# First loads, gate products and value loads of a windowed attention in front of a mixture of experts: another order

## The chip, the cores and the metric

One core of one Trainium2 chip. The metric is the device time of one execution in microseconds (us). TensorE (PE; PEld is its weight load), VectorE (DVE), ScalarE (ACT), GpSimd (POOL) and SyncE (SP) each run their instructions in program order; SP issues all direct loads and stores of the stage that is changed. About 1% of the time is what a measurement of this kernel can tell from no change.

## The reference, cut to what matters

```python
scores = scale * np.matmul(q, k.transpose(0, 1, 3, 2))     # 8 batches, 8 heads, 576 positions, 64 per head
mask = (rel >= 0) & (rel < 64)                             # each position sees the 64 last ones
attn = softmax(np.where(mask, scores, -1e9))
x = np.matmul(attn, v)                                     # as 4608 tokens x 512
...
do_compute = x @ w_skip > 0
e_idx = np.argmax(x @ w_gate, axis=1)                      # one of 8 experts; gate_w is its softmax
y = gate_w * (np.maximum(x @ w1[e_idx], 0) @ w2[e_idx])    # per token
out = x + y where do_compute, else x
```

## The kernel before

The tokens are cut into 36 tiles of 128 (two blocks of 64 positions of one batch, or the ninth blocks of two batches). A loop over t = 0 to 36 with an order written out by hand (`tc.manual_schedule`) interleaves the steps of several tiles. What round t puts on the engines, in this order: the loads that `at[t]` names (SP); `score(t + 1)` (PE: 4 band matmuls, line 214, that put the mask into PSUM, then 32 small q·k matmuls, line 228); the gate steps that `gate_at[t]` names; `soften(t)` (DVE maximum, line 243, and subtraction, line 244, then the exponential on ACT, line 245); `tile_out(t - 2)`, which is `av_tile` (PE: 32 matmuls, line 338; DVE: four operations, lines 350 to 358; SP: stores, two tiles later); `transpose_p(t - 1)` (PE: 8 transposes, line 254; ACT: two copies, line 255); and the ACT copies that `lower_at[t]` names (line 316). `routes(1)`, three times a round, puts out steps of the choice of experts, which runs in groups of 8, 8, 6, 8, 4 and 2 tiles. Score tiles (`psc`) and the softmax tiles (`sp`) have two buffers each, and so has the PSUM tag "t" that transposes and gate products share.

Loads come in 16 groups n of two tiles; `first_of[n]` is the first tile of group n: 0, 2, 4, 6, 9, 11, 13, 15, 18 and so on (after every eight tiles there is one of ninth blocks, with loads of its own, the tails). A group is q (512 KiB), k (512 KiB, 640 for odd n), vT (512 KiB: v transposed, for the gate products) and vm (592 KiB: v for the weighted sum, with room for gate columns). Before, q and k of group n are issued at round first_of - 5 (`AHEADQ`), vT and vm at first_of - 4 (`AHEADV`), from n = 2 and n = 1 on; what would fall before round 0 is issued there. vT has two buffers (`NTB`), the others four.

The gate steps of a group: `gate_v(n)` multiplies vT with the gate weights (PE, line 288, then an ACT copy, line 290) at round first_of - 2; `gate_vt(n)` transposes that product (PE, line 296), copies it into vm (ACT, line 308), and lets POOL copy the upper half of vm down for the block before (line 309), at first_of - 1; `lower` copies what is left of it on ACT, at first_of - 1 and, for odd n, at first_of. Rounds 0 and 1 hold what would come earlier. `tile_out` of the group's first tile stands in round first_of + 2. The tails have a product, a transposition and two such copies at rounds 9m + 4 to 9m + 7.

Ahead of the loop stand the first loads, in this order (KiB): k and q of the first block pair 128 + 128, identb 32, band 64, the next 128 + 128, ident 64, wg 64, then vT of group 0 (512), vm of group 0 (592), the rest of group 0's k and q (256 + 256), k and q of group 1 (640 + 512), two constants (180 and 305). Round 0 adds group 1's vT and vm, group 2's vT and vm, and group 2's k and q.

After the loop, the tokens of each expert are gathered and two matrix products per expert run with operands split in two parts each (lines 655 to 657).

Of the kernel before, what the change touches and what calls it, by code (L numbers as in the profile page):

```python
# [20 lines left out]
P = 128  # L21
# [21 lines left out]

NQB, NKB, NVB, NTB, NSB, NPB, XPB = 4, 4, 4, 2, 2, 3, 4

AHEADQ, AHEADV = 5, 4
SDELAY = 2

NRAW, NEARLY = 6, 2
# [76 lines left out]
def window_attention_moe(ctx: ExitStack, tc, a, out):  # L126
# [26 lines left out]
    def load_constants():  # L153
        nc.sync.dma_start(cf, a["c_f"])
        nc.sync.dma_start(lists, a["c_list"])
        nc.gpsimd.memset(onesb, 1.0)
        nc.gpsimd.tensor_copy(trib, cf[:, off["tri"]])
        nc.gpsimd.tensor_copy(base, cf[:, off["base"]])
        nc.gpsimd.tensor_copy(ent[:, :, 0].bitcast(I32), cf[:, off["tid"]])
# [19 lines left out]
    def load_qk(n, parts=((0, 4),)):  # L179
        b, g = divmod(n, 2)  # L180
        if parts[0][0] == 0:
            qs[n] = qkp.tile([P, 4, 4, 64], F32, name="q", bufs=NQB)
        q, k = qs[n], ks[n % NKB]
        for s, e in parts:
            s0 = s + 1 if s or not g else 0
            nc.sync.dma_start(k[:, s0 : e + 1], a["kT"][b, :, 4 * g + s0 - 1 : 4 * g + e])
            nc.sync.dma_start(q[:, s:e], a["qT"][b, :, 4 * g + s : 4 * g + e])
# [50 lines left out]
    def soften(t):  # L238
        ps = ss[t]
        s = sp.tile([P, 2 * 4, P], F32, name="s")  # L240
        flat = ps.rearrange("p r h k -> p (r h) k")
        mx = sm.tile([P, 8], F32, name="mx", bufs=2)
        nc.vector.tensor_reduce(mx, flat, axis=AX.X, op=ALU.max)  # L243
        nc.vector.tensor_tensor(s, flat, mx.unsqueeze(2).to_broadcast([P, 8, P]), op=ALU.subtract)  # L244
        nc.scalar.activation(s, s, AF.Exp, scale=0.125)  # L245
        ss[t] = s

    def transpose_p(t):
        s = ss.pop(t)
        ptm = ptp.tile([P, 8, P], F32, name="ptm")  # L250
        for r in range(2):
            pt = psum.tile([P, 4, P], F32, name="pt", tag="t", bufs=2)
            for p in range(4):
                nc.tensor.transpose(pt[:, p], s[:, 4 * r + p], ident)  # L254
            nc.scalar.copy(ptm[:, 4 * r : 4 * r + 4], pt)  # L255
        pts[t] = ptm
# [2 lines left out]
    banks = {}  # L259
    vms = {}  # L260

    def load_v(n):


        b, g = divmod(n, 2)
        vm = vp.tile([P, 4, H, VW], F32, name="vm", bufs=NVB)
        vT = vtp.tile([P, 4, 256], F32, name="vT")
        nc.sync.dma_start(vT, a["vT"][b, g])
        nc.sync.dma_start(
            vm.rearrange("p (j z) h c -> p j z (h c)", z=2)[:, :, 1], a["vp"][b, :, 2 * g : 2 * g + 2]  # L270
        )
        if g == 0:
            nc.gpsimd.memset(vm[:64, 0], 0.0)
        vms[n] = vm, vT

    def load_v_tail(m):
        vt = vp.tile([P, 2, H, VW], F32, name="vt", bufs=1)
# [6 lines left out]
    def gate(vT, nt):  # L284

        pw = psum.tile([P, nt * P], F32, name="pw", tag="t", bufs=2, padded_shape=[P, 512])
        for p in range(4):
            nc.tensor.matmul(pw[32 * p : 32 * p + 32], wg[:, p], vT[:, p], start=True, stop=True)
        vw = vtp.tile([P, nt * P], F32, name=f"vw{nt}")
        nc.scalar.copy(vw, pw)  # L290
        return vw

    def gate_t(vw, nt):
        pk = psum.tile([P, nt, P], F32, name="pk", tag="t", bufs=2, padded_shape=[P, 4, P])
        for j in range(nt):
            nc.tensor.transpose(pk[:, j], vw[:, j * P : j * P + P], ident)
        return pk.rearrange("p n (h c) -> p n h c", c=16)[..., 0:9]

    def gate_v(n):
        vms[n] = vms[n][0], gate(vms[n][1], 2)  # L300

    def gate_vt(n):

        b, g = divmod(n, 2)
        vm, vw = vms[n]
        pg = gate_t(vw, 2)
        w = vm.rearrange("p (j z) h c -> p j z h c", z=2)
        nc.scalar.copy(w[:, :, 1, :, 65:74], pg)  # L308
        nc.gpsimd.tensor_copy(w[64:, :, 0], w[:64, :, 1])  # L309
        for j in range(2):  # L310
            vs[9 * (n // 4) + 2 * (n % 4) + j] = [vm[:, 2 * j], vm[:, 2 * j + 1]]

    def lower(n, j):

        before = vms[n][0][64:, 1] if j else vms[n - 1][0][64:, 3]
        nc.scalar.copy(vms[n][0][:64, 2 * j], before)

    def gate_tail(m):
        vms["t", m] = vms["t", m][0], gate(vms["t", m][1], 1)
# [6 lines left out]
        vs[9 * m + 8] = [vt[:, 0], vt[:, 1]]  # L326

    def tail_lower(m, z):
        nc.scalar.copy(vms["t", m][0][:64, z], vms[4 * m + 2 * z + 1][0][64:, 3])

    def av_tile(t, lh, sums):
        blks = tiles[t]
# [200 lines left out]
    def routes(n):  # L533

        for _ in range(n):
            if not late:
                return
            if held[0] == "sums":
                held[1] += 1
                if progress[0] < NT or held[1] < 3:  # L540
                    continue
            held[:] = next(late[0], late), 0
            if held[0] is late:
                late.pop(0)
# [247 lines left out]
    with tc.manual_schedule():  # L792
        load_qk(0, ((0, 1),))
        nc.sync.dma_start(identb, a["c_identb"])
        nc.sync.dma_start(band, a["c_band"])
        load_qk(0, ((1, 2),))
        nc.sync.dma_start(ident, a["c_ident"])
        nc.sync.dma_start(wg, a["wg"])
        load_v(0)
        load_qk(0, ((2, 4),))  # L800
        load_qk(1)
        load_constants()
        at = {}

        def when_at(t, f, n):
            at.setdefault(max(t, 0), []).append((f, n))

        gate_at, lower_at = {}, {}
        for n in range(NG):
            if n >= 1:  # L810
                when_at(first_of[n] - AHEADV, load_v, n)
            if n >= 2:
                when_at(first_of[n] - AHEADQ, load_qk, n)
            gate_at.setdefault(max(first_of[n] - 2, 0), []).append((gate_v, n))
            at_t = max(first_of[n] - 2, 0) + 1
            gate_at.setdefault(at_t, []).append((gate_vt, n))
            lower_at.setdefault(at_t, []).append((lower, n, 1))
            if n % 2:
                lower_at.setdefault(at_t + 1, []).append((lower, n, 0))
# [8 lines left out]
        for t in range(NT + 1):  # L828
            m, r = divmod(t, 9)
            for f, n in at.get(t, ()):  # L830
                f(n)
            if t + 1 < NT:
                score(t + 1)
            for f, n in gate_at.get(t, ()):
                f(n)
            rest = its[0].split(*xhl[0], XSPLIT.index(t), "t") if t in XSPLIT else None
            routes(1)
            if t < NT:
                soften(t)
            if t >= 2 and t < NT:  # L840
                tile_out(t - 2)
            if rest is not None:
                rest()
            routes(1)
            if t >= 1 and t < NT:
                transpose_p(t - 1)
            routes(1)
            for f, n, j in lower_at.get(t, ()):
                f(n, j)
            for _ in range(U0.count(t)):  # L850
                weight_dma_first()
            if t in USPLIT:
                weight_split(ptr["split"])
                ptr["split"] += 1
# [245 lines left out]
```

## Time and profile before

| what | value |
|---|---|
| time, median of 3 runs | 479.13 us (475.76 to 481.17) |
| the profiled execution's own time | 476.28 us |
| its span, first to last instruction | 474.6 us |
| busy share of PE, DVE, ACT, POOL | 88%, 63%, 46%, 26% |
| moved by DMA | 99.61 MB |

The profile is one execution. Busy shares are means over a stage of attention (to about 205 us), which is where the change lies, and a stage of experts behind it. Times in rows count from the first instruction. A row of the order of time gives start, duration, engine, line, operation, out<-in, count, and in brackets how long the engine was idle before it and what ended that.

### The profile page before, as it was taken

What the parts mean: (1) busy time and instruction counts of PE and PEld (TensorE: products, weight loads), DVE (VectorE), ACT (ScalarE), POOL (GpSimd) and SP (SyncE); (2) the same over time, 40 slices, a digit from 0 to 9 for tenths busy, and PEclk for the clock granted to TensorE, in tenths of its full rate; (3) what the DMA queues carried; (4) which work ended last, traced back from release to release, by engine and by line L of the source; (5) the groups of instructions that cost most, each with busy time, mean ns of one, the idle gap of its engine ahead of it and who ended that gap; (6) DMA issues with size and microseconds to landing.
All of it is one profiled execution on the core that took longest, in us unless ns stands there. A gap on an engine that the chain in (4) does not pass through costs nothing.

```text
span 474.6 us, 11307 instructions
## 1 busy us (share of the span) xinstructions
PE 418.2 (88%) x4510; PEld 344.8 (73%) x4510; DVE 299.4 (63%) x562; ACT 220.3 (46%) x365; POOL 124.5 (26%) x139
## 2 busy tenths in 40 slices
PE   2899887987988688487999999999999999999990
PEld 2577774875766566376899888898888889988660
DVE  2478974896696788479833658847365476656510
ACT  1387554754674466467313444443334244444410
POOL 4210226024407141503456302305005030101010
PEclk9999988898999799799999999999999999999997
DMA  7999999859994984458573662746447555755000
GB/s 240 402 374 412 344 316 278 275 199 231 260 385 127 309 312 126 61 187 237 157 239 72 226 220 68 273 133 205 165 144 246 162 178 191 233 189 175 0 27 18
DMA packets 36646, 99.61 MB, mean 210 GB/s; under 512 B 6014, under 2 KB 8062, under 8 KB 36576
## 3 DMA queue, kind: packets, MB, share of 16 engines
q1 hardware_dynamic: 31728, 89.25, 57.6%
q0 software_dynamic: 4864, 9.63, 5.9%
q8 instruction: 36, 0.59, 0.5%
q14 instruction: 18, 0.15, 0.1%
HBM read 84.76 MB, written 14.73 MB: 210 GB/s over the span
## 4 chain that ended last, share of the span: by engine, by line
PE 60%; DVE 9%; ACT 3%; issue 3%; another core or an unknown queue 2%; POOLq 0%; DVEq 0%; ACTq 0%
PE p L655 8%; PE p L657 8%; PE p L656 8%; PE yw L655 4%; PE yw L656 4%; PE yw L657 4%; PE av L338 3%; PE yv L655 3%; PE yv L657 3%; PE yv L656 3%; PE pt L254 2%; PE ps L228 2%; DVE wlo L608 2%; PE px L644 2%; PE yu L657 2%
## 5 line engine op out<-in xcount | busy, mean ns | idle before, releaser
L608 DVE TENSOR_TENSOR wlo<-raw,whi 128x1024 fp32r<-128x1024 f32 x72 | 87.7, 1222 | 17.6 <-ACT whi L607 15.9
L692 ACT ACTIVATE hh<-p 128x256 fp32r<-128x256 f32 (+6 forms) x72 | 27.7, 385 | 129.7 <-PE p L657 116.9
L655 PE MATMUL p<-xh,whi 128*128 128x256 f32 (+6 forms) x288 | 84.5, 294 | 1.6 <-DVE gds L432 1.1
L657 PE MATMUL p<-xh,wlo 128*128 128x256 f32 (+6 forms) x288 | 83.7, 291 | 0.7 <-DVE wlo L608 0.7
L656 PE MATMUL p<-xl,whi 128*128 128x256 f32 (+6 forms) x288 | 83.7, 290 | 0.1
L607 ACT CAST whi<-raw 128x1024 fp32r<-128x1024 f32 x72 | 74.4, 1043 | 0.0
L693 DVE SCALAR_TENSOR_TENSOR hl<-p,hh 128x256 fp32r<-128x256 f32 (+6 forms) x72 | 30.3, 420 | 69.9 <-ACT hh L692 62.5
L715 POOL DMA_INDIRECT out<-yo,les x18 | 18.8, 1046 | 156.2 <-DVE yo L714 143.7
L655 PEld LDWEIGHTS p<-xh,whi 128*128 128x128 f32 x288 | 54.5, 189 | 4.9 <-issue 1.3
L656 PEld LDWEIGHTS p<-xl,whi 128*128 128x128 f32 x288 | 54.5, 189 | 1.8 <-issue 0.4
L657 PEld LDWEIGHTS p<-xh,wlo 128*128 128x128 f32 x288 | 54.6, 189 | 0.9 <-DVE wlo L608 0.9
L245 ACT ACTIVATE s<-s 128x1024 f32<-128x1024 f32 x36 | 38.1, 1058 | 36.8 <-DVE s L244 32.5
L440 POOL DMA_INDIRECT lists<-ent,gdi x36 | 37.0, 1029 | 67.2 <-DVE gdi L438 58.6
L338 PEld LDWEIGHTS av<-vm,ptm 128*64 128x64 f32 x1024 | 40.2, 149 | 19.3 <-issue 11.7
L243 DVE TENSOR_REDUCE mx<-ps 128x8 f32<-128x1024 f32 x36 | 43.8, 1216 | 15.5 <-PE ps L228 15.5
L338 PE MATMUL av<-vm,ptm 128*64 128x74 f32 x1024 | 46.1, 246 | 8.5 <-issue 5.6
L228 PE MATMUL ps<-k,q 64*64 64x128 f32 x1024 | 44.8, 294 | 9.6 <-issue 5.6
L255 ACT COPY ptm<-pt 128x512 f32<-128x512 f32 x72 | 38.9, 584 | 23.2 <-remote 14.9
L228 PEld LDWEIGHTS ps<-k,q 64*64 64x64 f32 x1024 | 36.3, 146 | 16.6 <-issue 10.1
L244 DVE TENSOR_TENSOR s<-ps,mx 128x1024 f32<-128x1024 f32 x36 | 44.1, 1225 | 5.6 <-ACT s L245 0.8
L254 PE MATMUL pt<-ident,s 128*128 128x128 f32 x288 | 41.2, 285 | 3.1 <-ACT ptm L255 2.9
L309 POOL COPY vm<-vm 64x1184 f32<-64x1184 f32 x16 | 18.7, 1172 | 72.1 <-ACT vm L308 66.9
(150 smaller groups left out, 672.2 us busy)
## 6 DMA issues: line engine op xcount, KB each, us to landing
raw<-wq SPq DMA_DIRECT2D x72, 512.0 KB
vm<-vp SPq DMA_DIRECT2D x16, 592.0 KB
vT<-vT SPq DMA_DIRECT2D x16, 512.0 KB
out<-x SPq DMA_DIRECT2D x32, 256.0 KB
q<-qT SPq DMA_DIRECT2D x15, 512.0 KB
k<-kT SPq DMA_DIRECT2D x8, 640.0 KB
k<-kT SPq DMA_DIRECT2D x7, 512.0 KB
kt<-kT SPq DMA_DIRECT2D x8, 256.0 KB
```

The costliest lines, as they stand in the source:

```text
L228: nc.tensor.matmul(ps[64 * hf : 64 * hf + 64, r, p], q[h, p], k[h, :, p], start=False, stop=p == 3, skip_group_check=True,)
L243: nc.vector.tensor_reduce(mx, flat, axis=AX.X, op=ALU.max)
L244: nc.vector.tensor_tensor(s, flat, mx.unsqueeze(2).to_broadcast([P, 8, P]), op=ALU.subtract)
L245: nc.scalar.activation(s, s, AF.Exp, scale=0.125)
L254: nc.tensor.transpose(pt[:, p], s[:, 4 * r + p], ident)
L255: nc.scalar.copy(ptm[:, 4 * r : 4 * r + 4], pt)
L338: nc.tensor.matmul(av[64 * hf : 64 * hf + 64, h // 4, (h % 4) * VW : (h % 4 + 1) * VW], ptm[:, (h % 2) * 4 + h // 2, 64 * hf : 64 * hf + 6 ...
L607: nc.scalar.copy(hi, raw)
L608: nc.vector.tensor_tensor(lo, raw, hi.bitcast(F32), op=ALU.subtract)
L655: nc.tensor.matmul(o, lh, rh, start=first, stop=False)
L656: nc.tensor.matmul(o, lh, rl, start=False, stop=False)
L657: nc.tensor.matmul(o, ll, rh, start=False, stop=last)
```

## The change

The first loads are put in another order: the rest of group 0's q and k comes ahead of ident, wg and vT; group 1's q and k are loaded in two halves, in front of vm of group 0 and behind it; group 1's vT and vm follow. The POOL steps that prepare constants for the choice of experts move from the head to round 4. `gate_v` and `gate_vt`, with their `lower` copies, come a round later for every group; in round 0 they stand behind `soften`, in round 1 behind `transpose_p`, from round 2 on where they stood. From group 2 on vT and vm are issued a round later (first_of - 3).

```diff
--- before.py
+++ after.py
@@ -43,7 +43,7 @@
 
 NQB, NKB, NVB, NTB, NSB, NPB, XPB = 4, 4, 4, 2, 2, 3, 4
 
-AHEADQ, AHEADV = 5, 4
+AHEADQ, AHEADV = 5, 3
 SDELAY = 2
 
 NRAW, NEARLY = 6, 2
@@ -153,6 +153,8 @@
     def load_constants():
         nc.sync.dma_start(cf, a["c_f"])
         nc.sync.dma_start(lists, a["c_list"])
+
+    def set_constants():
         nc.gpsimd.memset(onesb, 1.0)
         nc.gpsimd.tensor_copy(trib, cf[:, off["tri"]])
         nc.gpsimd.tensor_copy(base, cf[:, off["base"]])
@@ -259,19 +261,27 @@
     banks = {}
     vms = {}
 
-    def load_v(n):
-
-
+    def load_vT(n):
+        b, g = divmod(n, 2)
+        vT = vtp.tile([P, 4, 256], F32, name="vT")
+        nc.sync.dma_start(vT, a["vT"][b, g])
+        vTs[n] = vT
+
+    def load_vm(n):
         b, g = divmod(n, 2)
         vm = vp.tile([P, 4, H, VW], F32, name="vm", bufs=NVB)
-        vT = vtp.tile([P, 4, 256], F32, name="vT")
-        nc.sync.dma_start(vT, a["vT"][b, g])
         nc.sync.dma_start(
             vm.rearrange("p (j z) h c -> p j z (h c)", z=2)[:, :, 1], a["vp"][b, :, 2 * g : 2 * g + 2]
         )
         if g == 0:
             nc.gpsimd.memset(vm[:64, 0], 0.0)
-        vms[n] = vm, vT
+        vms[n] = vm
+
+    def load_v(n):
+        load_vT(n)
+        load_vm(n)
+
+    vTs, vws = {}, {}
 
     def load_v_tail(m):
         vt = vp.tile([P, 2, H, VW], F32, name="vt", bufs=1)
@@ -297,13 +307,13 @@
         return pk.rearrange("p n (h c) -> p n h c", c=16)[..., 0:9]
 
     def gate_v(n):
-        vms[n] = vms[n][0], gate(vms[n][1], 2)
+        vws[n] = gate(vTs.pop(n), 2)
 
     def gate_vt(n):
 
         b, g = divmod(n, 2)
-        vm, vw = vms[n]
-        pg = gate_t(vw, 2)
+        vm = vms[n]
+        pg = gate_t(vws.pop(n), 2)
         w = vm.rearrange("p (j z) h c -> p j z h c", z=2)
         nc.scalar.copy(w[:, :, 1, :, 65:74], pg)
         nc.gpsimd.tensor_copy(w[64:, :, 0], w[:64, :, 1])
@@ -312,8 +322,8 @@
 
     def lower(n, j):
 
-        before = vms[n][0][64:, 1] if j else vms[n - 1][0][64:, 3]
-        nc.scalar.copy(vms[n][0][:64, 2 * j], before)
+        before = vms[n][64:, 1] if j else vms[n - 1][64:, 3]
+        nc.scalar.copy(vms[n][:64, 2 * j], before)
 
     def gate_tail(m):
         vms["t", m] = vms["t", m][0], gate(vms["t", m][1], 1)
@@ -326,7 +336,7 @@
         vs[9 * m + 8] = [vt[:, 0], vt[:, 1]]
 
     def tail_lower(m, z):
-        nc.scalar.copy(vms["t", m][0][:64, z], vms[4 * m + 2 * z + 1][0][64:, 3])
+        nc.scalar.copy(vms["t", m][0][:64, z], vms[4 * m + 2 * z + 1][64:, 3])
 
     def av_tile(t, lh, sums):
         blks = tiles[t]
@@ -794,11 +804,14 @@
         nc.sync.dma_start(identb, a["c_identb"])
         nc.sync.dma_start(band, a["c_band"])
         load_qk(0, ((1, 2),))
+        load_qk(0, ((2, 4),))
         nc.sync.dma_start(ident, a["c_ident"])
         nc.sync.dma_start(wg, a["wg"])
-        load_v(0)
-        load_qk(0, ((2, 4),))
-        load_qk(1)
+        load_vT(0)
+        load_qk(1, ((0, 2),))
+        load_vm(0)
+        load_qk(1, ((2, 4),))
+        load_v(1)
         load_constants()
         at = {}
 
@@ -807,12 +820,11 @@
 
         gate_at, lower_at = {}, {}
         for n in range(NG):
-            if n >= 1:
-                when_at(first_of[n] - AHEADV, load_v, n)
             if n >= 2:
                 when_at(first_of[n] - AHEADQ, load_qk, n)
-            gate_at.setdefault(max(first_of[n] - 2, 0), []).append((gate_v, n))
-            at_t = max(first_of[n] - 2, 0) + 1
+                when_at(first_of[n] - AHEADV, load_v, n)
+            gate_at.setdefault(max(first_of[n] - 1, 0), []).append((gate_v, n))
+            at_t = max(first_of[n] - 1, 0) + 1
             gate_at.setdefault(at_t, []).append((gate_vt, n))
             lower_at.setdefault(at_t, []).append((lower, n, 1))
             if n % 2:
@@ -831,12 +843,17 @@
                 f(n)
             if t + 1 < NT:
                 score(t + 1)
-            for f, n in gate_at.get(t, ()):
-                f(n)
+            gates = gate_at.get(t, ())
+            if t > 1:
+                for f, n in gates:
+                    f(n)
             rest = its[0].split(*xhl[0], XSPLIT.index(t), "t") if t in XSPLIT else None
             routes(1)
             if t < NT:
                 soften(t)
+            if t < 1:
+                for f, n in gates:
+                    f(n)
             if t >= 2 and t < NT:
                 tile_out(t - 2)
             if rest is not None:
@@ -844,6 +861,11 @@
             routes(1)
             if t >= 1 and t < NT:
                 transpose_p(t - 1)
+            if t == 1:
+                for f, n in gates:
+                    f(n)
+            if t == 4:
+                set_constants()
             routes(1)
             for f, n, j in lower_at.get(t, ()):
                 f(n, j)
```

## Rows read from the trace of the kernel before

**Rows 1.** The page of the profile: the span, and the busy tenths of PE (matmul) in 40 slices of 11.9 us; then two of the groups of instructions, with count, busy us and mean ns of one, idle us before them and what ended it: the scatters of the choice of experts, and POOL's copy of vm.

```profile
span 474.6 us, 11307 instructions
...
PE   2899887987988688487999999999999999999990
...
L440 POOL DMA_INDIRECT lists<-ent,gdi x36 | 37.0, 1029 | 67.2 <-DVE gdi L438 58.6
...
L309 POOL COPY vm<-vm 64x1184 f32<-64x1184 f32 x16 | 18.7, 1172 | 72.1 <-ACT vm L308 66.9
```

**Rows 2.** The head of the kernel in order of time. The matmuls of line 228 are those of score(0) (4.99), score(1) (11.91) and score(2) (18.47); line 243 and line 244 at 7.55 and 8.81 are soften(0), line 245 at 18.45 its exponential; line 288 at 17.03 is the gate product of group 1; line 338 at 24.08 is the weighted sum of tile 0.

```profile
4.99 2.31 PE L228 MATMUL ps<-k,q 64*64 64x128 f32 x30
...
7.55 1.23 DVE L243 TENSOR_REDUCE mx<-ps 128x8 f32<-128x1024 f32 x1 [7.55 <-PE ps L228]
...
8.81 1.22 DVE L244 TENSOR_TENSOR s<-ps,mx 128x1024 f32<-128x1024 f32 x1
...
11.91 1.98 PE L228 MATMUL ps<-k,q 64*64 64x128 f32 x32 [3.96 <-DMA q<-qT]
...
17.03 1.08 PE L288 MATMUL pw<-vT,wg 128*32 128x256 f32 x8 [2.13 <-DMA vT<-vT]
...
18.45 1.06 ACT L245 ACTIVATE s<-s 128x1024 f32<-128x1024 f32 x1
18.47 1.92 PE L228 MATMUL ps<-k,q 64*64 64x128 f32 x32
...
24.08 1.25 PE L338 MATMUL av<-vm,ptm 128*64 128x74 f32 x32
```

**Rows 3.** Busy time of each engine in ten stretches of 3 us: stretch, its length, busy us and instructions of PE, PEld, DVE, ACT and POOL, then PE's granted clock, the busy share of the 16 DMA engines and GB/s moved.

```profile
0.00:3.00 3.00, 0.00 (x0) 0.00 (x0) 0.00 (x0) 1.28 (x1) 2.33 (x10) 1.00 0.26 81
3.00:6.00 3.00, 1.39 (x17) 1.18 (x20) 0.00 (x0) 0.00 (x0) 3.00 (x7) 1.00 0.81 188
6.00:9.00 3.00, 1.94 (x31) 1.27 (x24) 1.41 (x2) 0.00 (x0) 0.31 (x2) 1.00 0.87 311
9.00:12.00 3.00, 0.09 (x4) 0.12 (x8) 1.04 (x1) 0.00 (x0) 0.00 (x0) 1.00 1.04 389
12.00:15.00 3.00, 2.90 (x40) 1.69 (x40) 1.05 (x1) 0.03 (x1) 0.00 (x0) 1.00 1.03 417
15.00:18.00 3.00, 0.97 (x8) 0.20 (x8) 1.40 (x2) 0.34 (x1) 1.11 (x4) 1.00 1.04 403
18.00:21.00 3.00, 3.00 (x44) 2.31 (x40) 0.53 (x1) 1.40 (x3) 0.00 (x0) 1.00 1.00 388
21.00:24.00 3.00, 2.84 (x54) 1.98 (x52) 1.92 (x2) 2.98 (x7) 2.30 (x2) 1.00 1.01 400
24.00:27.00 3.00, 3.00 (x68) 2.60 (x68) 1.55 (x5) 2.98 (x6) 0.00 (x0) 1.00 1.02 402
27.00:30.00 3.00, 3.00 (x66) 2.48 (x54) 2.77 (x5) 1.83 (x4) 1.62 (x2) 1.00 1.03 278
```

**Rows 4.** Issues on SP's queue in order of time: the last of group 0's q, vm of group 1, vT of group 2, k of group 4, the first k of the tail.

```profile
6.11 0.46 SPq L187 DMA_DIRECT2D q<-qT  x1
...
10.45 0.38 SPq L269 DMA_DIRECT2D vm<-vp  x1
14.96 0.33 SPq L268 DMA_DIRECT2D vT<-vT  x1
...
25.04 0.33 SPq L186 DMA_DIRECT2D k<-kT  x1
...
28.93 0.33 SPq L194 DMA_DIRECT2D kt<-kT  x1
```

**Rows 5.** What SP's queue waited for in the first 40 us: who, for whom, us in total, times, longest.

```profile
SPq L194 <- DMA q<-qT: 1.9, 1, 1.9
```

**Rows 6.** The beat of the rounds, in order of time on PE: the band matmuls with which score(3) to score(9) begin, and the gate product of group 3, which waits for its vT.

```profile
22.29 0.41 PE L214 MATMUL ps<-band,identb 64*64 64x512 bf16 x4
...
26.28 0.41 PE L214 MATMUL ps<-band,identb 64*64 64x512 bf16 x4
...
30.07 0.41 PE L214 MATMUL ps<-band,identb 64*64 64x512 bf16 x4
...
31.71 0.64 PE L288 MATMUL pw<-vT,wg 128*32 128x256 f32 x8 [0.35 <-DMA vT<-vT]
...
34.49 0.41 PE L214 MATMUL ps<-band,identb 64*64 64x512 bf16 x4
...
38.64 0.41 PE L214 MATMUL ps<-band,identb 64*64 64x512 bf16 x4
...
42.33 0.41 PE L214 MATMUL ps<-band,identb 64*64 64x512 bf16 x4
...
46.32 0.41 PE L214 MATMUL ps<-band,identb 64*64 64x512 bf16 x4
```

**Rows 7.** In order of time: a lower copy on ACT that ends round 6, and the weighted sum of round 7, the next on PE.

```profile
43.71 0.68 ACT L316 COPY vm<-vm 64x592 f32<-64x592 f32 x1
...
44.11 1.25 PE L338 MATMUL av<-vm,ptm 128*64 128x74 f32 x32
```

**Rows 8.** In order of time, later in the attention: a weighted sum at the slower pace, and an operation of DVE behind a long wait.

```profile
62.98 2.21 PE L338 MATMUL av<-vm,ptm 128*64 128x74 f32 x32
...
80.35 0.17 DVE L350 TENSOR_SCALAR r<-av 128x8 f32<-128x8 f32 x1 [5.68 <-remote]
```

## The prediction, made before the change was run

> **What bounds the kernel now.** The page comes first: PE fills nearly every slice from the twentieth on, and until then has holes [rows 1]. The change lies in the attention, so the question is what a gain there is worth at the end. All engines run in program order, and behind the attention PE works without a hole; what the head gains and nothing takes back arrives at the end in full.
>
> The head is read next, in order of time [rows 2]. soften(0) is subtracted by 8.81 + 1.22 = 10.03, yet its exponential starts at 18.45: in round 0 the gate products of groups 0 and 1 stand ahead of it on ACT, and the second waits for its vT until 17.03. score(1) waits 3.96 us for the rest of q, until 11.91. The first weighted sum starts at 24.08.
>
> Then the DMA engines by stretches [rows 3]: from 9 to 30 us they are busy all the time, at 388 to 417 GB/s, but for one stretch of 278. So the loads are a second bound, hardly below the first: the order decides what comes early, not how much has come by then.
>
> Last the rounds [rows 6]. Band matmuls of successive scores lie 3.99 (round 2, a gate product), 3.79 (a gate transposition), 4.42 (a product that waits 0.35 for its vT), 4.15, 3.69 and 3.99 us apart, with PE busy 3.00 of 3.00 us in some stretches [rows 3].
>
> **How arrivals are reckoned.** SP issues in order, and at most eight loads are under way: the wait named for the tail's k is a q [rows 5], eight issues back. So an issue time tells a landing: k of group 4 was issued at 25.04, so q of group 2 had landed; the tail's first k at 28.93, so q of group 3 had [rows 4]. Bytes moved are sums of [rows 3] (times 3 us): 4158 kB by 15 us, 6531 by 21, 7731 by 24. vT of group 1 stands at 4501 KiB (4610 kB) of the order and landed at 17.03, with 4976 kB moved, 366 behind; q of group 2 stands at 7221 KiB (7395 kB) and landed at 25.04 with 8149 moved, 754 behind. I carry 366 kB up to 17 us and 754 after.
>
> **The change, part by part.** *First loads.* In the new order the rest of q of group 0 ends at 1120 KiB, vT 0 at 1760, the first half of k and q of group 1 at 2400, the second half at 3504, vT 1 at 4016, vm 1 at 4608, q of group 2 at 6117, its vT at 6629. By the rule above they land at 8.3, 10.1, 11.8, 15, 15.8, 17.3, 22.2 and 23.5 us.
>
> score(1) then runs from 8.3 to 10.3 (1.98 us, from its row), not from 11.91. The exponential of tile 0 runs at 10.05, 8.4 us earlier, since the gate products now stand behind it. score(2) waits for its halves until 11.8 and takes 1.92 (18.47 before), so 13.8; the transposes of tile 0 (8 at the slower pace, about 1.4) end at 15.2; gate_v(1) waits for vT 1 until 15.8 and takes 1.08; score(3) starts at 16.9 instead of 22.29 [rows 6]. That is 5.4 us. The added wait is this one, in round 1: behind it on PE stand score(3) and the first weighted sum, and on ACT the copy of the product and the exponential of tile 2.
>
> Round 2 costs 3.8 (it has a transposition): score(4) could start at 20.7, but q of group 2 lands at 22.2. The vT of group 2 (23.5) then lets its product end at 24.1, the weighted sum (1.25) at 25.4, the transposes at 26.4: score(5) starts at 26.4, 3.7 us before its 30.07. Round 4 has a transposition, 3.8: score(6) at 30.2. In round 5 vT 3 is needed at 31.6; its place in the order (9437 KiB) is the same in both kernels, and it landed by 31.71: a wait of 0.1. With product and tail product together the round takes 4.35, then 4.05 with both transpositions (both estimates: a round without gates about 3.45, from 4.15 and 3.99 less the added matmuls), then 3.69: score(9) at 42.3 instead of 46.32. So of 5.4 us about 4.0 is left, because q and vT of group 2 can't come earlier. The tail's k and q keep their place too (to 11821 KiB, 12105 kB): with 9771 kB moved by 30 us and 400 GB/s they land at 37.7, and score(8) needs them at 38.6.
>
> *Splitting k and q of group 1* adds two loads on SP (0.46 each, rows like 6.11 [rows 4]), under the transfers in front of them. That the stream runs at 389 to 417 GB/s with eight loads under way [rows 3] speaks for no price.
>
> The Trainium skill ("DMA: Bandwidth & Descriptors", section Bandwidth) advises loads of 1 MiB or more, and its section on the anatomy of one DMA gives each a fixed 2.0 us, measured for loads that GpSimd issues; two more loads in series would cost 4 us by it and take the gain. The trace disagrees for loads that overlap: 512 KiB loads kept 400 GB/s.
>
> *vT a round later.* SP issued nothing from 10.45 to 14.96: it waited for the product that frees a vT buffer, k and q of group 2 behind it [rows 4]. Now these come first. From round 3 on the lead stays: vT two rounds ahead of its product, vm three ahead of the transposition.
>
> *Constants on POOL.* The two constant loads stay with SP; four small POOL steps go to round 4, five rounds ahead of the first use. POOL has nothing pressing there: 1.62 us busy of 3 [rows 3]. Nothing; if the cover went, 1 us.
>
> *Gates a round later, for good.* Three effects. First, in each nine rounds the tail's product now meets a group's product, and one round has no gate at all. That round can't fall below DVE's 3.69, while the full ones cost PE's sum: 12.1 against 11.85, 0.25 lost; once is in the 42.3 above, three times more is 0.75. Second, the weighted sum of an odd group's first tile now follows one round after `lower`. The row shows it: that copy ends at 43.71 + 0.68 = 44.39, while the weighted sum of the next round started at 44.11 [rows 7], 0.28 late; other rounds have 0 to 0.1. Seven such places: 0 to 2.0, I take 0.35, near the other rounds, since DVE has some slack to swallow it. Third, rounds 32 and 33 hold the first expert's transposes as well, on the two PSUM buffers of tag "t"; the last group's transposition joins round 33: 0 to 1.0, I take 0.3. POOL's copy of vm has one round less of lead but still 1.5 rounds, some 6 us, against its own 1.17 and the three scatters of 1.03 [rows 1] that a round can put ahead of it: nothing.
>
> **Sum.** 4.0 - 0.75 - 0.35 - 0.3 = 2.6 us. The profiled execution took 476.28; 473.7 would be its counterpart. It was faster than two of the three runs; on the median, 479.13 - 2.6 = 476.5. The runs spread by 5.4, and 1% (4.8 us) is about what a measurement here can tell from no change.
>
> **Rivals.** *The whole 5.4 us arrives, or more.* If loads lag less than 754 kB (at 366, q and vT of group 2 land 1 us earlier), and the beat has the slack to hide the later gates. For it: DVE, not PE, bounds some rounds. Against it: vT 3 is at 31.7 either way. Time: 479.13 - 5.4 = 473.7, and 472 when a stall like the 5.68 us one [rows 8] falls better. Chance 0.2.
>
> *The loads take everything.* The change doesn't do what it says if the DMA stream is the sole bound until 45 us. For it: DMA share 1.0 through 30 us. Against it: behind the product at 31.71 no row of the beat waits for a load [rows 6]. Time 479 to 478. Chance 0.13.
>
> *Slower: the weighted sum waits for `lower`.* In the seven rounds after an odd group's second copy PE stands until ACT is done, and score, transposes and DVE behind it. It decides the sign from (4.0 - 0.75 - 0.3) / 7 = 0.42 us each; at 0.8 each, where the slow rounds put the exponential late, 5.6 are lost and the time is 479.13 - 2.95 + 5.6 = 481.8. For it: 0.28 in [rows 7], and PE is full there. Against it: most rounds show 0.1. Chance 0.08.
>
> *PE's clock.* score(1) and score(2) took 1.98 and 1.92 us, and the weighted sum 1.25 at 24.08 [rows 2] but 2.21 at 62.98 [rows 8]: the head is at the pace of the 1.2 GHz level, though the column reads 1.00, and the faster pace came after PE had been busy without a break from 18 to 21 [rows 3]. If the new gaps in the head, above all the 1.5 us for q of group 2, keep it low through rounds 2 and 3, each takes some 7 us instead of 3.8 (matmuls nearly doubled): score(5) at 30.9 instead of 30.07, so 0.8 + 1.4 slower, 481.3. Against it: between 11.8 and 20.7 PE has hardly a gap. Chance 0.05.
>
> The Trainium skill ("TensorE: Matmul & The Clock Gate", part 1) calls the low clock the default, which activity releases; the pace of the head agrees, and by that rule gaps for loads are what this rival needs.
>
> **How the numbers follow.** The forecast (gain 1 to 4.5 us) has 0.54; the others 0.2, 0.13, 0.08, 0.05. Its own range is 474.5 to 478.2. To hold 8 in 10 the range reaches from 472 to 480.5: it leaves out the slower rivals and the best of the first. Faster by over 1% is the first rival and a little of the forecast, 0.26; slower by over 1% (over 483.9) the worst of the last two, 0.06; else 0.68.
>
> **What the new profile would show.** Exponential of tile 0 near 10, score(3) near 17, score(4) waiting for q of group 2 until about 22, score(5) near 26.4 and score(9) near 42.3; line 338 waiting for line 316 by 0.1 to 0.3 us in seven rounds. Wrong would be: score(9) before 41 (loads lag less) or after 44 (they bound it, or the clock), or a gain at score(9) that is gone by 205 us.

## The result: slower, by 0.4 to 0.9 per cent

The changed kernel took 482.81 us (median of 20 runs, 480.17 to 488.65), the kernel before beside it 478.63 (475.62 to 483.08): a ratio of 1.0094, 95% interval 1.0065 to 1.0123. Run again on one chip (a1_after_again, below) it was 480.8 against 478.04, ratio 1.0035 (1.000 to 1.007); the two intervals just overlap. The forecast was 476.5, with a range that ended at 480.5, and a gain.

The profiled execution took 482.46 us. Its page: span, PE in 40 slices of 12.0 us, and the groups that answer to [rows 1], with that of the weighted sum (count, busy us and mean ns of one, idle us before them and what ended it).

```profile
span 480.8 us, 11313 instructions
...
PE   4899879977978788288899999999999999999990
...
L348 PE MATMUL av<-vm,ptm 128*64 128x74 f32 x1024 | 47.2, 246 | 14.5 <-issue 13.7
...
L450 POOL DMA_INDIRECT lists<-ent,gdi x36 | 37.1, 1030 | 58.8 <-DVE gdi L448 47.3
...
L319 POOL COPY vm<-vm 64x1184 f32<-64x1184 f32 x16 | 18.7, 1170 | 97.2 <-ACT vm L318 90.9
```

PE is fuller in the first slices (4899 against 2899) and emptier in the seventeenth (2 against 4; 192 to 204 us). In front of the weighted sum PE idles 14.5 us, 9.30 of them in one place (tile 33, below); in the kernel before the same group has 8.5.

The head of the changed kernel in order of time, answering to [rows 2]: line 247 at 10.65 is the exponential of tile 0, lines 230 at 13.17 and 22.90 the matmuls of score(2) and score(4), line 298 at 17.59 the gate product of group 1.

```profile
10.65 1.06 ACT L247 ACTIVATE s<-s 128x1024 f32<-128x1024 f32 x1 [8.48 <-DVE s L246]
...
13.17 1.95 PE L230 MATMUL ps<-k,q 64*64 64x128 f32 x32 [0.64 <-DMA q<-qT]
...
17.59 0.64 PE L298 MATMUL pw<-vT,wg 128*32 128x256 f32 x8 [0.30 <-ACT ptm L257]
...
19.75 1.25 PE L348 MATMUL av<-vm,ptm 128*64 128x74 f32 x32
...
22.90 1.10 PE L230 MATMUL ps<-k,q 64*64 64x128 f32 x32 [0.54 <-DMA q<-qT]
```

The beat, answering to [rows 6]: the band matmuls that begin score(3), score(5), score(6) and score(9), and the gate product of group 3.

```profile
18.16 0.41 PE L216 MATMUL ps<-band,identb 64*64 64x512 bf16 x4
...
26.91 0.41 PE L216 MATMUL ps<-band,identb 64*64 64x512 bf16 x4
...
30.70 0.41 PE L216 MATMUL ps<-band,identb 64*64 64x512 bf16 x4
...
32.62 0.64 PE L298 MATMUL pw<-vT,wg 128*32 128x256 f32 x8 [0.64 <-DMA vT<-vT]
...
42.94 0.41 PE L216 MATMUL ps<-band,identb 64*64 64x512 bf16 x4
```

score(3) begins 4.1 us earlier than before, score(5) 3.2, score(9) 3.4. So the head did nearly what was reckoned, and the gain was there at 43 us. It was gone at the first expert: the first `hh` (line 702) starts at 210.87 us, before it was 205.86. From there to the end both kernels take much the same (269.9 and 268.7). The loss lies between tile 9 and the end of the attention, and most of it late: by the start of DVE's maximum (line 245, before line 243) the changed kernel is 2.4 us ahead at tile 9, 3.2 ahead at tile 30 and 2.1 behind at tile 33.

Then the place that answers to [rows 7]: ACT and PE around the weighted sum of tile 6, the first tile of group 3.

```profile
43.40 1.05 ACT L257 COPY ptm<-pt 128x512 f32<-128x512 f32 x2
...
44.15 0.64 PE L298 MATMUL pw<-vT,wg 128*32 128x256 f32 x8
...
44.46 0.68 ACT L326 COPY vm<-vm 64x592 f32<-64x592 f32 x1
45.05 0.68 ACT L339 COPY vt<-vm 64x592 f32<-64x592 f32 x1
45.25 1.25 PE L348 MATMUL av<-vm,ptm 128*64 128x74 f32 x32 [0.46 <-issue]
```

`lower` (line 326) stands behind the two copies of ptm and ends at 45.14 by its rounded row; 0.1 us later the weighted sum starts. PE had nothing to do from 44.79 on. The row calls this 0.46 us "issue"; what tells the releaser is that the same distances come back at five of the eight odd groups: in the changed kernel the weighted sums of tiles 6, 11, 15, 24 and 33 all start 0.79 to 0.80 us after the last copy of ptm and 0.10 after `lower`. At the other three (tiles 2, 20, 29) PE is busy until the sum starts. The four rows behind tile 6, with the copies in front of the last:

```profile
72.60 2.24 PE L348 MATMUL av<-vm,ptm 128*64 128x74 f32 x32 [0.54 <-issue]
...
91.16 1.25 PE L348 MATMUL av<-vm,ptm 128*64 128x74 f32 x32 [0.42 <-issue]
...
140.14 1.25 PE L348 MATMUL av<-vm,ptm 128*64 128x74 f32 x32 [0.17 <-issue]
...
198.86 0.59 ACT L257 COPY ptm<-pt 128x512 f32<-128x512 f32 x1 [4.73 <-remote]
...
201.57 0.68 ACT L326 COPY vm<-vm 64x592 f32<-64x592 f32 x1
...
202.35 2.24 PE L348 MATMUL av<-vm,ptm 128*64 128x74 f32 x32 [9.30 <-issue]
```

Of the 9.30 us at tile 33 `lower` has some 0.8; the rest is that both copies of ptm come late.

Two theories were set up. A: the gates a round later cost the time, in the rounds. B: the long stalls in which PE and DVE stand while GpSimd scatters (the 5.68 us of [rows 8]) fell worse by chance.

### The profile page after: what moved, and what is told of

It is laid out like the page before. It is cut to its first block, busy times and chain, and to the rows that moved or that the text cites. A ratio compares the mean times of both kernels' runs of the same rounds, so it can differ in the third digit from the quotient of the medians.

```text
span 480.8 us, 11313 instructions
## 1 busy us (share of the span) xinstructions
PE 420.5 (87%) x4510; PEld 350.2 (73%) x4510; DVE 300.1 (62%) x562; ACT 219.8 (46%) x365; POOL 125.2 (26%) x139
## 4 chain that ended last, share of the span: by engine, by line
PE 64%; DVE 9%; DMA 4%; issue 4%; ACT 3%; another core or an unknown queue 2%; POOLq 0%; SPq 0%; DVEq 0%; ACTq 0%
PE p L667 8%; PE p L665 8%; PE p L666 7%; PE av L348 5%; PE pt L256 4%; PE yw L665 4%; PE yw L666 4%; PE yw L667 4%; PE yv L665 3%; PE ps L230 3%; PE yv L667 3%; PE yv L666 3%; DMA vt<-vpt 2%; DVE s L246 2%
## 5 line engine op out<-in xcount | busy, mean ns | idle before, releaser
L348 PE MATMUL av<-vm,ptm 128*64 128x74 f32 x1024 | 47.2, 246 | 14.5 <-issue 13.7
L450 POOL DMA_INDIRECT lists<-ent,gdi x36 | 37.1, 1030 | 58.8 <-DVE gdi L448 47.3
L230 PEld LDWEIGHTS ps<-k,q 64*64 64x64 f32 x1024 | 37.3, 149 | 16.4 <-issue 13.8
L256 PE MATMUL pt<-ident,s 128*128 128x128 f32 x288 | 44.3, 300 | 2.4 <-ACT ptm L257 2.2
L319 POOL COPY vm<-vm 64x1184 f32<-64x1184 f32 x16 | 18.7, 1170 | 97.2 <-ACT vm L318 90.9
```

What stands on the lines that cost most here:

```text
L230: nc.tensor.matmul(ps[64 * hf : 64 * hf + 64, r, p], q[h, p], k[h, :, p], start=False, stop=p == 3, skip_group_check=True,)
L348: nc.tensor.matmul(av[64 * hf : 64 * hf + 64, h // 4, (h % 4) * VW : (h % 4 + 1) * VW], ptm[:, (h % 2) * 4 + h // 2, 64 * hf : 64 * hf + 6 ...
```

## The experiments

**Each part alone, and both kernels without the scatters** (on one chip, kernel before 478.89). e1_head_only has the new first loads, and the old rounds for the gates from group 2 on; e2_gates_only has the old first loads, and the later gates. The two others leave out the scatters of the choice of experts.

```
e1:  -            gate_at.setdefault(max(first_of[n] - 1, 0), []).append((gate_v, n))
     +            late_by = 1 if n < 2 else 2
     +            gate_at.setdefault(max(first_of[n] - late_by, 0), []).append((gate_v, n))
     and AHEADV back to 4
e2:  the same lines in the kernel before, with late_by = 2 if n < 2 else 1, AHEADV 3
e3, e4:  -            ins = nc.gpsimd.indirect_dma_start(out=lists, ...)
```

> The new order of first loads and the gates behind the softmax in rounds 0 and 1 are kept; from group 2 on gate products, lower copies and value loads stand in the rounds of before. Theory A (the gates a round later cost the time, in every nine rounds and most in rounds 31 to 35): the head's gain of 3 to 4 us stays, 474.5 to 476.5, score(9)'s softmax 3 us earlier than before and still 2 us earlier at round 30. Theory B (stalls of PE under POOL's scatters and gathers grow by chance of where the earlier head puts them): the time is near that of the changed kernel, 481 to 484, with the head's gain there at round 20 and gone by round 35.

> The head of before; from group 2 on gate products, lower copies and value loads a round later, as in the changed kernel. Theory A: 479 plus 5 to 8, so 484 to 487, the loss coming in rounds 26 to 36. Theory B: near before, 477 to 481, since nothing moves the rounds.

> The changed kernel without the 36 scatters into the lists (the experts then find empty lists, gathers and output scatters move nothing). Theory B: without the scatters the stalls of PE in rounds 13 to 35 go, and this kernel is 2 to 4 us faster than the next one. Theory A: it is still 2 to 5 us slower than the next one, since the gates' places are the same.

> The kernel before without the 36 scatters into the lists, as the yardstick for the kernel ahead. Both theories: some 10 to 20 us faster than before, as its stalls under the scatters (5.7 us at 80, 3.6 at 115, 2.7 at 151, 6 from 190 to 198) go.

Measured: e1 480.2 (ratio 1.0001, 0.9968 to 1.0033), e2 484.97 (1.0095, 1.0061 to 1.0128), e3 452.81 (0.9463, 0.9413 to 0.9512), e4 448.34 (0.9369, 0.9325 to 0.9413). The changed kernel is 4.5 us slower without any scatter too, so the loss doesn't need the scatters, and B falls as its whole cause; GpSimd's gathers are still in e3 and e4 (below). The later gates alone cost 4.6 us, so A stands. e1 is no clean test of the head, as its trace shows (the gate product of group 2):

```profile
23.41 1.08 PE L298 MATMUL pw<-vT,wg 128*32 128x256 f32 x8 [4.55 <-DMA vT<-vT]
```

In the old round that product asks for vT of group 2 before it has landed, and PE stands 4.55 us: in the head the later gate belongs to the new loads. (It also dates the landing: 23.4, reckoned 23.5.)

**The small copies spread, without scatters.** The change put `lower(n, 0)` of an odd group at the end of the round just ahead of the weighted sum that reads it, and twice in nine rounds it put a `lower` beside a tail_lower that was left in place. n1 moves `lower(n, 0)` two rounds up and one tail_lower a round up; n2 moves the tail's gate steps a round later as well; n3 is the changed kernel with groups 4 to 15 in their old rounds; h1 is n3 with its scatters, the whole computation.

```
n1:  -                lower_at.setdefault(at_t + 1, []).append((lower, n, 0))
     +                lower_at.setdefault(at_t - 1 if n > 1 else at_t + 1, []).append((lower, n, 0))
     -            lower_at.setdefault(9 * m + 4, []).append((tail_lower, m, 0))
     +            lower_at.setdefault(9 * m + 3, []).append((tail_lower, m, 0))
n2:  also gate_tail at 9 * m + 6, gate_tail_t at 9 * m + 7
n3, h1:  -            gate_at.setdefault(max(first_of[n] - 1, 0), []).append((gate_v, n))
         +            early = 2 if n >= 4 else 1
         +            gate_at.setdefault(max(first_of[n] - early, 0), []).append((gate_v, n))
         and load_v at first_of[n] - AHEADV - (n >= 4)
```

> The changed kernel without the scatters (left out: GpSimd's writes of the entry lists, so the experts work on an empty list), with the small ACT copies spread: an odd group's first `lower` two rounds earlier and the first tail_lower one round earlier, so that no round but the fourth has two of them. Its pairs so far: 452.8 us for the changed kernel without scatters, 448.3 for the kernel before without them. If two such copies in one round, ahead of the weighted sum that needs the second, are what the later gates cost (1.4, 1.0 and 1.1 us longer beats in rounds 5, 6 and 8, 2.1 in round 31): 447 to 450. If they are not: 452 to 454.

> As the one above (no scatters either), and the tail's gate product and transposition a round later too, so that the rounds carry the same gate steps in the same order as in the kernel before, all one round later. If the cost of the later gates is only the pile-up of steps that the change moved against steps that it left in place: the head's gain of 3 to 4 us arrives, 444.5 to 446. If it is the shorter lead itself: 450 to 453.

> The changed kernel without scatters, but groups 4 to 15 have their v loads and gate steps in the rounds of the kernel before; only groups 0 to 3 stay a round later. If the loss comes from the later gates of rounds 10 to 35: about 448.3 - 1.7 (what was left of the lead at round 9 in the pair without scatters) = 446.6, range 445 to 447.5. If a lead of the head is lost behind round 9 in any case: 448 to 450.

> The same with its scatters, the whole computation. By the first theory 478.6 - 1.7 to 3.5 = 475 to 477; by the second 478.6 to 480.

Measured (kernel before 478.53): n1 449.82 (0.9375, 0.9333 to 0.9417), n2 451.48 (0.9429, 0.9381 to 0.9476), n3 449.3 (0.9378, 0.9337 to 0.942), h1 476.1 (0.994, 0.991 to 0.997). Against e3, n1 takes 0.9 of a per cent back, some 4 us. Taking the two products apart as well (n2) brings nothing more; its time is the one expected if the shorter lead itself costs. n3 lies where a head's lead that is lost anyway would put it, but its interval (446.8 to 450.8 us) reaches the other theory too, and its scattering twin h1, which was timed twelve times, decides for the first. h1 is faster than both kernels: the head's gain is real where the later gates go no further than group 3.

**The same on the whole kernel, and the last groups.** f1_lowers is n1 with the scatters. h2 is h1 with the copies and the tail's steps of the first nine rounds spread. n4 is n1 with groups 12 to 15 in the old rounds.

> The changed kernel, whole, with the small ACT copies spread as in n1_no_scatter_lowers (an odd group's first `lower` two rounds earlier, the first tail_lower one round earlier). If the piled-up copies cost as much beside the scatters as without them (ratio 0.9463 against 0.9375, 4.2 us of 478.5): 482.8 - 4.2 = 478.6, range 477 to 480. If the stalls beside GpSimd's scatters decide instead: 481 to 484.

> h1_old_from_4 (groups 4 to 15 as in the kernel before) with the copies and the tail's gate steps of the first nine rounds spread as well (group 3's first `lower` two rounds earlier, the first tail_lower one round earlier, the first tail's product and transposition one round later). h1's lead shrank from 4.3 us at tile 3 to 1.0 at tile 9; if the pile-up of rounds 4 to 8 took it: 1 to 2 us below h1, 474 to 475.5. If the loads took it: as h1, 476 to 477.

> n1_no_scatter_lowers (no scatters, copies spread), with groups 12 to 15 in the rounds of the kernel before, v loads too. In n1's profile 4.1 us went from round 30 to round 34, in n3's (all groups from 4 on in the old rounds) none. If that is the later gates among the first expert's transposes: 446 to 447.5 and a lead of 1 to 2 us over the kernel before (without scatters) still there at tile 35. If it is where the gather happens to fall: 449 to 451.

On the chip of these three runs the kernel before took 459.63 us, 19 less than elsewhere, so ratios alone are compared. f1 454.89 (0.9898, 0.9855 to 0.9941): faster. h2 456.94 (0.9976, 0.9939 to 1.0012): no better than h1 (0.994), against what was expected; the edit shows no gain in the first nine rounds. n4 446.01: 3.8 us below n1, though on another chip, and in its profile the lead holds through the last rounds.

**Four kernels on one chip** (kernel before 478.04): the changed kernel unaltered, f1, f4 (n4 with its scatters) and h1.

> The changed kernel again, unaltered, beside three variants of it on one chip: runs of the kernel before differed between chips (478.5 and 459.6 us), so ratios of one chip are wanted. If the later gates cost it everywhere: 1.003 to 1.011 times the time of the kernel before on this chip. If the stalls beside the scatters decide: 1.005 to 1.011 where the kernel before takes 478 us, and 0.990 to 0.997 where it takes 460.

> f1_lowers again (the changed kernel with the small ACT copies spread), beside the changed kernel itself. If the piled-up copies are the larger part of the cost: 0.006 to 0.010 below the ratio of a1_after_again. If not: within 0.003 of it.

> f1_lowers with groups 12 to 15 in the rounds of the kernel before (n4_no_scatter_old_from_12 with its scatters, the whole computation). n4 kept its lead through the last rounds, 3.8 us below the kernel n1. If both causes add up: 0.006 below f1 and 0.012 to 0.018 below the changed kernel. If the last rounds' stalls eat it: as f1.

> h1_old_from_4 again (only groups 0 to 3 a round later), beside the others. It gave 0.994 on a chip where the kernel before took 478.5. If that is the part of the head's lead that outlives tile 9: 0.992 to 0.997 here as well; f4 below it by 0.003 or more if the old rounds matter only at the end of the attention.

Measured: a1 480.8 (1.0035, 1.000 to 1.007), f1 475.85 (0.9936, 0.9895 to 0.9976), f4 476.38 (0.9956, 0.9926 to 0.9986), h1 475.79 (0.9927, 0.989 to 0.9964). The copies are worth 0.0099, 4.7 us (2 to 7 by the two intervals); f1's gain of 3.1 us is about the 2.6 that was forecast. f4 is no better than f1: what the last groups give without scatters (n4) doesn't show in the times beside them.

**Which of the two edits.** s1 and s2 move only both tail_lower steps a round later (to rounds 5 and 8 of nine): no round has two small copies, but `lower(n, 0)` stays late. s2 is without scatters.

```
     -            lower_at.setdefault(9 * m + 4, []).append((tail_lower, m, 0))
     -            lower_at.setdefault(9 * m + 7, []).append((tail_lower, m, 1))
     +            lower_at.setdefault(9 * m + 5, []).append((tail_lower, m, 0))
     +            lower_at.setdefault(9 * m + 8, []).append((tail_lower, m, 1))
```

> The changed kernel with only the two tail_lower steps of each nine rounds a round later (rounds 5 and 8 of the nine), so that no round has two small ACT copies, while an odd group's first `lower` stays where the change put it, one round ahead of the weighted sum that needs it. The changed kernel: 1.0035 and 1.0094 times the kernel before; with both edits (f1_lowers) 0.9936 and 0.9898. If two copies in one round are the cost: 0.990 to 0.997. If it is the weighted sum that waits for the late first `lower`: 1.002 to 1.009.

> The same without the scatters (left out as in e3_after_no_scatter). e3: 452.8 us; with both edits (n1_no_scatter_lowers) 449.8. If two copies in one round are the cost: 448 to 450.5. If the late first `lower` is: 451.5 to 454.

Measured (kernel before 478.13): s1 479.96 (1.0039, 1.001 to 1.0068), s2 453.41 (0.9466, 0.9425 to 0.9506): as the changed kernel (1.0035) and as e3 (0.9463). So two copies in one round alone don't cost it; what f1 has beyond s1 is the earlier `lower(n, 0)`. Tile 6 in s1, in order of time:

```profile
43.54 1.05 ACT L257 COPY ptm<-pt 128x512 f32<-128x512 f32 x2
...
44.61 0.68 ACT L326 COPY vm<-vm 64x592 f32<-64x592 f32 x1
...
45.39 0.83 PE L348 MATMUL av<-vm,ptm 128*64 128x74 f32 x19 [0.42 <-issue]
```

and in f1 (f1_lowers_again), whose `lower(3, 0)` ran two rounds ahead, at 36.55 (that of 40.84 is `lower(3, 1)`, which s1 has at 40.86), and where a tail_lower that this sum doesn't read has its place:

```profile
36.55 0.68 ACT L326 COPY vm<-vm 64x592 f32<-64x592 f32 x1
...
40.84 0.68 ACT L326 COPY vm<-vm 64x592 f32<-64x592 f32 x1
...
43.56 1.06 ACT L257 COPY ptm<-pt 128x512 f32<-128x512 f32 x2
...
44.64 0.68 ACT L339 COPY vt<-vm 64x592 f32<-64x592 f32 x1
44.88 1.10 PEld L348 LDWEIGHTS av<-vm,ptm 128*64 128x64 f32 x32 [0.41 <-issue]
44.88 1.25 PE L348 MATMUL av<-vm,ptm 128*64 128x74 f32 x32
```

The copies of ptm end within 0.03 us of each other, the same ACT copy time follows, and the sum starts 0.51 us earlier where it doesn't read it.

## Why the prediction was wrong

*Right: the first loads.* score(3) at 18.16 (reckoned 16.9), score(4) waiting for q of group 2 until 22.90 (22.2), score(5) at 26.91 (26.4), score(6) at 30.70 (30.2), score(9) at 42.94 (42.3): 3.4 of the 4.0 us arrived. The lead was 4.1 us at score(3), where 5.4 was reckoned, and 3.2 at score(5), behind a wait of 0.54 for q of group 2, where 1.5 was reckoned. Reading landings from the issue queue and the bytes moved held to 0.7 us for q and vT of group 2; vT of group 3 came at 32.62, 0.9 after the 31.71 that was expected again. No price shows for the two added loads: the exponential of tile 0 runs at 10.65, as reckoned to 0.6.

*Wrong: the term "weighted sum follows one round after `lower`", 0.35 us for seven places.* f1 undoes it at seven places (odd groups from 3 on), moves one tail_lower in nine rounds as well, and regains 4.7 us, 0.67 a place on average. The mechanism and the number of places were in the text, and the rival "the weighted sum waits for `lower`" put 0.8 on each and 481.8 us on the whole; it got a chance of 0.08. With 4.7 the prediction's own sum gives 4.0 - 0.75 - 0.3 - 4.7 = -1.75, so 480.9; a1 measured 480.8, 2.8 above the kernel before on its chip by medians, 1.7 by the ratio. That is no second proof, since the 4.7 comes from a1 itself; it says the same as f1's gain of 3.1, close to the sum without this term (2.95). The 4.2 us of the first comparison are more than this sum explains. A gain at score(9) that is gone by 205 us was among the prediction's own signs of being wrong.

The error was in how [rows 7] was read. It compared the end of a copy with the start of a weighted sum that doesn't depend on it, got 0.28, and took most of that away because other rounds showed less. But what counts is where the copy's end lies once the sum waits: behind both copies of ptm, which are themselves the last thing that ACT finishes before the sum. That is the last ptm end + 0.68 + 0.10. By the same rows a sum that needs the copy of 43.71 starts at 44.49, 0.38 after 44.11: 2.7 us for seven places, not 0.35. Tile 6 shows 0.51.

The waits that the trace shows directly come to less than 4.7: 0.46, 0.54, 0.42, 0.17 and some 0.8 at tile 33, 2.4 us in all. The rest is not traced. Two things differ beside it. The waits named "remote" (last section), those of ACT and DVE from 60 to 215 us added up, are 40.8 to 47.3 us in the profiles of the changed kernel, a1, e2 and s1, and 31.0 to 40.4 in the six without the late copy behind group 3 (kernel before 31.0, f1 32.2). And PE's granted clock, the median over the runs, was 0.954 in a1, 0.957 in f1 and 0.960 in the kernel before on the same chip; in the first comparison the changed kernel had 0.947. Whether the late copy brings these along is open.

*Not shown: full rounds at 0.75.* n2 against n1 finds no gain from taking the two products apart.

*Wrong in the trace, open in the times: the last groups at 0.3.* The starts of DVE's maximum cut the attention into stretches (us, one execution each):

| kernel | start, tile 9 | tile 9 to 30 | tile 30 to 33 | tile 33 to first `hh` |
|---|---|---|---|---|
| before | 50.4 | 115.1 | 15.9 | 24.5 |
| changed | 48.0 | 114.3 | 21.1 | 27.5 |
| f1 (again) | 47.4 | 112.6 | 19.6 | 25.2 |
| f4 | 48.4 | 114.3 | 16.8 | 24.2 |
| e4, before without scatters | 50.6 | 95.1 | 15.5 | 18.7 |
| e3, changed without scatters | 48.9 | 97.3 | 18.7 | 19.2 |
| n1 | 47.9 | 96.4 | 19.4 | 18.9 |
| n4 | 47.2 | 96.7 | 14.7 | 19.3 |

From tile 30 to tile 33 all ten profiled kernels whose groups 12 to 15 come a round later take 17.2 to 21.2 us, the nine others 14.7 to 16.8. It follows that edit: n4 differs from n1, and f4 from f1, in these groups and the tail_lower among them alone. So the stretch costs 3 to 5 us more, not 0.3, and holds most of what the changed kernel lost behind tile 9. What the prediction left out there is POOL's queue: in the old rounds POOL's copy of vm lies between the second and the third of the first expert's four gathers, in all nine kernels; a round later it comes behind the fourth, in all ten, and in seven of these ten a weighted sum beside the gathers takes 3.9 to 5.8 us, in two (n2, s2) a score 4.2 and 3.1; in the nine such a sum takes 2.5 at most (rows in the last section). What the stretch is worth in the time of the whole kernel is not shown: n4 is 3.8 us below n1, but on another chip; on one chip f4 and h1 are no faster than f1, nor n3 than n1. In f1 tiles 9 to 30 take 2.5 us less than in the kernel before, which makes up for most of it; why is open.

*The rival on PE's clock happens in some executions.* In 5 of 15 profiles of kernels with the new first loads and the later gate of group 2 the granted clock fell between 23 and 33 us, and the softmax of tile 9 began at 49.9 to 51.5 us; in the other ten at 47.2 to 49.4. The trace of a1 shows it best: score(2), score(4), then two stretches (columns as in [rows 3]).

```profile
12.47 1.10 PE L230 MATMUL ps<-k,q 64*64 64x128 f32 x32 [0.63 <-DMA q<-qT]
...
23.21 2.28 PE L230 MATMUL ps<-k,q 64*64 64x128 f32 x32 [1.95 <-DMA q<-qT]
...
21.00:24.00 3.00, 1.05 (x16) 0.67 (x15) 2.57 (x4) 1.28 (x3) 0.00 (x0) 0.91 1.02 411
24.00:27.00 3.00, 3.00 (x46) 1.86 (x42) 0.00 (x0) 0.41 (x2) 0.00 (x0) 0.52 1.04 394
```

Here PE was early enough to stand 1.95 us for q of group 2, and right after that it ran at the 1.2 GHz level: 2.28 us for score(4) instead of 1.10, and score(5) began at 28.82, 1.9 later than above. It is the gap that the rival named, at its place, though the clock didn't stay low, as the rival had it: it had risen (1.10 us for score(2)) and fell again. The chance of 0.05 was too low.

*POOL's copy of vm was put at nothing.* Besides its place among the gathers, it has a price where DVE meets it. The pair is e3 and e4, the same operation of one round with and without the copy beside it:

```profile
89.45 1.17 POOL L319 COPY vm<-vm 64x1184 f32<-64x1184 f32 x1 [10.80 <-ACT vm L318]
89.48 1.22 DVE L416 TENSOR_TENSOR goh<-gfi,gfm 128x64 f32<-128x64 f32 x1
```

```profile
92.61 0.23 DVE L406 TENSOR_TENSOR goh<-gfi,gfm 128x64 f32<-128x64 f32 x1
```

1.0 us, in a round that DVE bounds. The kernel before meets it too, in another round (56.38, also 1.22), so moving the copy by a round moves the collisions; the runs don't price the difference.

## What to carry to other kernels

When a step is moved nearer to the one that reads it, reckon its end from the queue it stands in (what its engine finishes just before, plus its own time), not from where the reader happened to start while it didn't wait, and multiply by every place. Move the whole chain of such small steps together: here the same change with `lower(n, 0)` issued two rounds earlier (and one tail_lower one round earlier) is 1% faster than as it was made, and 0.6% faster than the kernel before. A wait named "issue" that ends a fixed 0.1 us behind the same copy on another engine, place after place, points to that copy; move the copy, and see whether the distance goes. And look at what a moved step stood between: POOL's copy of vm had kept four gathers apart.

## What the runs showed of the hardware

**The waits beside the scatters differ from chip to chip.** The whole kernel before took 478 to 479 us in five groups of runs and 459.63 in one; f1 took 475.85 on a chip of the first kind and 454.89 on that one. The scatters themselves run alike (36 in 37.1 us in both profiles of f1); what differs is what waits beside them. The kernels without scatters took 446 to 453 us, but none of them ran on both kinds of chip. The waits from 60 to 200 us (who, for whom, us in total, times, longest) in f1, first where the kernel before took 478.04, then where it took 459.63:

```profile
ACT ptm L257 <- remote: 14.4, 7, 4.6
DVE r L360 <- remote: 11.8, 4, 5.6
PEld ps L230 <- issue: 10.9, 18, 1.2
```

```profile
PEld ps L230 <- issue: 2.0, 3, 0.9
```

Waits named "remote", for PE's results that come late, are in the first and not in the second. Their cause is open. The changed kernel itself was not run on that chip; f1 was, and its ratio of 0.9898 says that f1's gain needs no such stalls.

**PE can trickle while GpSimd gathers.** In n1, beside four gathers of rows of out, the weighted sum comes mostly in bursts of three to five matmuls, one every 0.74 us, and takes 4.9 us (the first of the gathers, then PE, then POOL's copy of vm):

```profile
148.41 1.07 POOL L477 DMA_INDIRECT xg<-out,es  x1 [2.78 <-DMA es<-lists]
...
150.46 0.37 PE L348 MATMUL av<-vm,ptm 128*64 128x74 f32 x4 [0.23 <-issue]
...
151.20 0.32 PE L348 MATMUL av<-vm,ptm 128*64 128x74 f32 x3 [0.38 <-issue]
...
151.94 0.40 PE L348 MATMUL av<-vm,ptm 128*64 128x74 f32 x5 [0.41 <-issue]
...
154.55 1.16 POOL L319 COPY vm<-vm 64x1184 f32<-64x1184 f32 x1 [1.12 <-ACT vm L318]
```

In n4 the copy stands behind the second gather, and the sum beside them takes 1.25 us:

```profile
148.95 1.03 POOL L477 DMA_INDIRECT xg<-out,es  x1 [0.30 <-issue]
...
149.34 1.25 PE L348 MATMUL av<-vm,ptm 128*64 128x74 f32 x32
...
149.99 1.18 POOL L319 COPY vm<-vm 64x1184 f32<-64x1184 f32 x1
...
151.34 1.02 POOL L477 DMA_INDIRECT xg<-out,es  x1 [0.17 <-issue]
```

In n2 it is a score beside the last gathers that comes in such bursts, from 151.22 to 155.42 us. On the chip of 459.63 f1 has the four gathers in a row too and shows one hole of 0.67 us. No row shows what PE waits for.

**DVE stands for the whole of a POOL copy.** goh reads two tiles of SBUF, and ends 0.08 us behind the copy (90.70 and 90.62). The Trainium skill ("SBUF — State Buffer", section "SBUF: two separate sides") says that such a VectorE operation and a GpSimd operation that reads SBUF hold a shared pair of ports exclusively, and the later one blocks for the whole instruction; the trace agrees, with 1.22 us beside the copy and 0.23 without.
